# A longer transfer time in the planner's queue model, a new load order, and ten spins ahead of the first transpose

## The chip, the cores and the metric

The kernel runs on one core of one Trainium2 chip. The metric is device time in microseconds (us). Four runs of the kernel before gave 297.55, 297.69, 298.71 and 296.12 us; the median is 297.62 us. A difference of about 1% is what a measurement of this kernel can tell from no change.

## The reference, cut to what matters

Two layers follow each other. The first is a linear recurrence over 768 steps for 4 sequences and 8 heads of 48 elements; the second is a mixture of four experts in which every expert runs on every row:

```python
for t in range(S):                       # r, k, v: (4, 8, 768, 48)
    cur   = einsum('bhd,bhe->bhde', u[None] * kt, vt)
    y[:, :, t] = einsum('bhd,bhde->bhe', rt, state + cur)
    state = w[None, :, :, None] * state + einsum('bhd,bhe->bhde', kt, vt)
x = y as rows: (3072, 384)
p = domain_probs / (domain_probs.sum(-1, keepdims=True) + 1e-09)
for e in range(4):                       # w1: (4, 384, 1024), w2: (4, 1024, 384)
    out += p[:, e:e+1] * (maximum(x @ w1[e], 0.0) @ w2[e])
```

## The kernel before

**Attention.** The 3072 rows are cut into 24 chunks of 128 rows. Chunk `ci` is step `ci // 4` of sequence `ci % 4`, so four neighbouring chunks (a block) belong to four sequences and only chunk `ci + 4` needs the state that chunk `ci` leaves. Each chunk loads three tiles, `Rt`, `Kt` and `Vt` (192 KB each, in rows of 192 bytes; below they are R5, K5, V5 for chunk 5). `scale` multiplies R and K by powers of `w` into `RK`; `T` transposes `RK` (on TensorE with a copy `Tout` for chunks 0 to 7, by a DMA transpose from SyncE's queue for the others); `At` multiplies the two (from chunk 8 on, two chunks at a time); `mask` cuts the triangle; `Y` forms the output from `At`, `Vb` (the bf16 copy of V) and the state; `Yout` adds `dv`, the part of `u`, which GpSimd computes by `ruk_a`, `ruk_b` (with VectorE's sum `dcoef`) and `dv`; `X` transposes the result into `xTe`, the input of the experts (chunks 0 to 7 on TensorE, the others by a DMA transpose `Xout`); `Sm`, `Sv` and `S` renew the state. TensorE's `l1` (lines 596 and 602) forms x @ w1 for a block of four chunks, ScalarE's `relu` (L611, L613) takes it out of PSUM, `l2` (L632) forms h @ w2 chunk by chunk, and `ev` (L640, L642) adds it to `oacc`.

**Weights.** Each of the eight weight matrices comes in three pieces, here `w1e2.0`, `w1e2.1`, `w1e2.2` (576, 576 and 384 KB of f32), is loaded into a slot `wst` and cast to bf16 (`cast`, by ScalarE, VectorE or GpSimd; lines 72 to 76). An `l1` group needs the piece that holds its columns; from the third slot on an `l2` needs all three.

**What sets the order.** No engine decides anything at run time. Each step is a job with an engine, a duration, the jobs that it needs and a rank. When the program is built, a planner (lines 686 to 840) plays the jobs through: an engine that is free takes the ready job of lowest rank. All engines then get their instructions in the planned order, and each engine works through its own queue strictly in that order, so a job whose input is late holds up what stands behind it. All loads, stores and DMA transposes are issued by SyncE, whose jobs are planned in the same way; loads are ranked by their place in the string `ORDER` (L219), which a program outside had searched. The function `dma()` (L690) models the queue behind SyncE: a transfer begins when the one before it has ended, and ends after its duration `us` (0.965 for an R, K or V tile, 0.555 for each 128 rows or columns of a weight piece, 1.1 and 0.45 for DMA transposes). Its result is the time from which the planner lets the jobs that need the transfer begin.

**Spins.** In the first 20 us the planner writes idle matmuls (`spin`, L173) into TensorE's queue. Between two TensorE jobs it puts as many as fit in the gap that the plan shows (L818). The plan gives the products `wmm` and `umm` (L261 and L265: rows of w and u spread over all partitions) 1.65 us each. The first transpose of chunk 0, job `("T", 0, 0)`, is the next job after `umm`; the plan shows no gap between them.

Of the kernel before, what the change touches and what calls it, by code (L numbers as in the profile page):

```python
# [19 lines left out]
def kernel(  # L20
# [129 lines left out]
    def job(name, on, run, needs=(), rank=0.0, takes=(), drops=(), moves=None,  # L150
            behind=()):
        j = Job()
        j.behind = behind
        j.name, j.on, j.run, j.needs, j.rank = name, on, run, list(needs), rank
        j.takes, j.drops, j.moves = takes, drops, moves
        for k in drops:
            tokens[k] = tokens.get(k, 0) + 1
        j.pad = 0.0
        ci = name[1] if isinstance(name, tuple) and name[0] in ATT else -1
        if ci >= SUB:  # L160

            j.pad = PAD_PE if "T" in on else PAD
        j.no = len(jobs)
        assert name not in jobs
        jobs[name] = j
# [3 lines left out]
    def spin(n, m=4):  # L169

        ps = psum.tile([128, 4, 128], F32, tag="mm", bufs=4, name="spin_ps")
        for _ in range(n):
            nc.tensor.matmul(ps[:, 0:m, :], spin_in, spin_in[:, None, :].to_broadcast((128, m, 128)),  # L173
                             start=True, stop=True)
# [40 lines left out]
    def load_p():  # L215
        load_job("prow", (0.36, 2), lambda: nc.sync.dma_start(
            prow, moe_domain_probs.rearrange("(n p) e -> n p e", p=C)))

    ORDER = ("K1 R1 K0 R0 V0 R2 K2 V1 w1e0.1 w1e0.2 K3 w1e0.0 R3 V2 w2e0.0 V3 w2e0.1 w2e0.2 p w1e1.2 "  # L219
             "w1e1.1 R4 w1e1.0 K5 K4 w2e1.0 w2e1.2 w2e1.1 R5 V4 w1e2.2 w1e2.1 K6 w1e2.0 V5 K7 w2e2.2 "  # L220
             "w2e2.1 w2e2.0 R6 V6 K8 V7 R7 w1e3.2 w1e3.0 K9 w1e3.1 w2e3.0 V9 R9 R8 V8 V11 V10 R11 "
             "K10 R10 K12 K11 w2e3.1 V12 w2e3.2 R13 R12 K13 V13 " +
             " ".join(f"c{i}" for i in range(14, TOTC))).split()
    for what in ORDER:
        if what == "p":
# [87 lines left out]
    def attention(ci):  # L313
        b, c = ci % B, ci // B
# [3 lines left out]
        rk = float(ci)  # L318
# [16 lines left out]
        us = 0.48 if ci < SUB else 0.65  # L335
# [33 lines left out]
        def dv():  # L369
            tl["dv", ci] = work.tile([128, H, D], F32, tag="dv", bufs=3, name="dv")  # L370
            nc.gpsimd.tensor_mul(tl["dv", ci], tl["Vt", ci],  # L371
                                 tl["dcoef", ci].to_broadcast((128, H, D)))
        job(("dv", ci), {"P": 0.82}, dv, [("dcoef", ci)], rk - 0.4, (("dv", ci),), (("inp", ci),))

        if dmat:
            def tr():
# [168 lines left out]
    for ci in range(TOTC):  # L545
        attention(ci)
# [136 lines left out]
    avail = {"T": 3.7, "V": 4.5, "A": 3.3, "P": 1.5, "S": 0.6}  # L683


    RING, DMA_LAG, DMA_END = 118, 1.67, 0.7
    queued = []
    expanded = [0.0]

    def dma(now, base, us, nd):  # L690

        taken = max(now + base, expanded[0])
        at = taken
        while True:
            live = [(b, f, n) for b, f, n in queued[-12:] if f > at]
            n_out = sum(n * min(1.0, (f - at) / (f - b)) for b, f, n in live)
            if not live or n_out + nd + 1 <= RING:
                break
            at += 0.05
        expanded[0] = at  # L700
        b = max(taken - base + DMA_LAG, at + 0.4, queued[-1][1] if queued else 0.0)
        queued.append((b, b + us, nd + 1))
        return taken, b + us + DMA_END
    ready_at = {j.name: 0.0 for j in jobs.values()}
    waiting = {e: [] for e in avail}
    events = []
# [15 lines left out]
    now, seq, n_done = 0.0, 1, 0  # L722
# [7 lines left out]
    def start(e):  # L730
# [34 lines left out]
        if j.moves:  # L765
            taken, end = dma(now, us, *j.moves)
            us = taken - now + 0.04
# [15 lines left out]
    while n_done < len(jobs):  # L783
        assert events, "no job can begin"
        now, _, what, x = heapq.heappop(events)
# [25 lines left out]
    with tc.manual_schedule(engines={ET.PE, ET.Pool, ET.DVE, ET.Activation, ET.SP}):  # L811
        spin(NSPIN)
        pe_end = 3.7
        for t, _, e, j in started:
            if e == "T":
                slow = 2.0 if t < 9.0 else 1.0
                n = int((t - pe_end - 0.1) / (0.056 * slow))
                if t < 20 and n > 0:  # L818
                    spin(n, 1)
                pe_end = t + j.on[e] * (2.0 if t < WARM and j.name not in ("wmm", "umm") else 1.0)  # L820
            if len(j.on) > 1 or j.name[0] in ("cast", "Vb", "Tout") or \
                    (j.name[0] == "Xout" and e in "VA"):
                j.run(e)
            else:
                j.run()
# [30 lines left out]
```

## Time and profile before

| | |
|---|---|
| time of the profiled execution | 297.55 us |
| its span, first to last instruction | 295.7 us (1.85 us lie around it) |
| median of four runs | 297.62 us (296.12 to 298.71) |
| TensorE (PE) busy | 285.8 us, 97% |
| weight loads on PE | 169.2 us, 57% |
| VectorE (DVE), ScalarE (ACT), GpSimd (POOL) busy | 153.3, 152.4, 102.9 us |
| granted clock | 1.000 |
| DMA share, 20 to 80 us | 0.96, at 256 GB/s |
| DMA share, 100 to 280 us | 0.34, at 74 GB/s |

A window line gives a stretch of the span, its length, the busy time of PE, of its weight loads, of DVE, ACT and POOL (with the number of instructions), the granted clock, the mean busy share of the 16 DMA engines and the GB/s. A timeline line gives start and duration in us, engine, line, operation, output and inputs, and in brackets how long the engine was idle before and what ended that. A line of waits gives who waited for whom: us in total, times, the longest. "SPq" is SyncE's queue issuing transfers.

### The profile page before, as it was taken

What the parts mean: (1) busy time and instruction counts of PE and PEld (TensorE: products, weight loads), DVE (VectorE), ACT (ScalarE), POOL (GpSimd) and SP (SyncE); (2) the same over time, 40 slices, a digit from 0 to 9 for tenths busy, and PEclk for the clock granted to TensorE, in tenths of its full rate; (3) what the DMA queues carried; (4) which work ended last, traced back from release to release, by engine and by line L of the source; (5) the groups of instructions that cost most, each with busy time, mean ns of one, the idle gap of its engine ahead of it and who ended that gap; (6) DMA issues with size and microseconds to landing.
All of it is one profiled execution on the core that took longest, in us unless ns stands there. A gap on an engine that the chain in (4) does not pass through costs nothing.

```text
span 295.7 us, 5781 instructions
## 1 busy us (share of the span) xinstructions
PE 285.8 (97%) x2264; PEld 169.2 (57%) x2293; DVE 153.3 (52%) x298; ACT 152.4 (52%) x251; POOL 102.9 (35%) x138
## 2 busy tenths in 40 slices
PE   7899999999979999999999999999999999999995
PEld 2787556868735555555555555555555555555553
DVE  5976778697474957536547436545414322101223
ACT  3775958754474443464543564444464444565440
POOL 3783243919849555443522453401000000000000
PEclk9999999999999999999999999999999999999999
DMA  7999889999989497392093383130340100200003
GB/s 151 288 304 298 259 263 304 220 254 192 237 162 177 82 201 179 105 196 46 17 172 88 109 166 70 28 71 29 90 89 0 27 2 27 80 2 0 0 2 106
DMA packets 111199, 37.66 MB, mean 127 GB/s; under 512 B 99242, under 2 KB 111148, under 8 KB 111172
## 3 DMA queue, kind: packets, MB, share of 16 engines
q1 hardware_dynamic: 111156, 37.29, 52.5%
q8 instruction: 18, 0.29, 0.5%
q14 instruction: 9, 0.07, 0.1%
q10 hardware_dynamic: 16, 0.00, 0.0%
HBM read 26.79 MB, written 4.72 MB: 107 GB/s over the span
## 4 chain that ended last, share of the span: by engine, by line
PE 81%; DMA 6%; SPq 6%; POOL 3%; issue 2%; DVE 1%; ACT 1%; POOLq 0%; DVEq 0%
PE out_ps L632 38%; PE hT_ps L602 31%; PE hT_ps L596 5%; SPq L191 4%; DMA wst<-in_moe_w_dram 3%; DMA Vt<-in_v_dram 2%; PE At_ps L436 2%; PE Y_ps L474 1%; DMA Rt<-in_r_dram 1%; PE Y_ps L467 1%; PE St_ps L515 1%; SPq L202 1%; POOL S L535 1%; POOL ruk L353 1%; PE RKT_ps L394 1%
## 5 line engine op out<-in xcount | busy, mean ns | idle before, releaser
L613 ACT ACTIVATE hTs<-hT_ps 128x512 bf16<-128x512 f32 x168 | 99.6, 597 | 94.4 <-PE hT_ps L602 89.4
L632 PE MATMUL out_ps<-w_sb,hTs 128*128 128x384 bf16 x760 | 138.9, 326 | 0.6 <-DVE oacc L642 0.4
L602 PE MATMUL hT_ps<-xTe,w_sb 128*128 128x512 bf16 x475 | 122.0, 379 | 3.0 <-ACT hTs L613 1.6
L632 PEld LDWEIGHTS <-hTs 128*128 128x128 bf16 x760 | 72.6, 98 | 53.7 <-issue 1.0
L642 DVE SCALAR_TENSOR_TENSOR oacc<-out_ps,p_nat,oacc 128x384 f32<-128x384 f32 x71 | 43.8, 617 | 89.8 <-PE out_ps L632 89.5
L602 PEld LDWEIGHTS <-w_sb 128*128 128x128 bf16 x504 | 47.1, 98 | 48.4 <-issue 1.8
L445 DVE TENSOR_TENSOR AtM<-At_ps,mask 128x512 bf16<-128x512 f32 x48 | 30.8, 682 | 16.3 <-PE At_ps L436 16.3
L345 POOL TENSOR_TENSOR ruk<-Rt,Kt 128x384 f32<-128x384 f32 x24 | 24.3, 1017 | 41.5 <-DMA Kt<-in_k_dram 28.7
L371 POOL TENSOR_TENSOR dv<-Vt,dcoef 128x384 f32<-128x384 f32 x24 | 20.4, 853 | 45.5 <-DVE Ysb L483 30.6
L353 POOL TENSOR_TENSOR ruk<-ruk,U_sd 128x384 f32<-128x384 f32 x23 | 23.4, 1020 | 0.9
L640 ACT ACTIVATE oacc<-out_ps,p_nat 128x384 f32<-128x384 f32 x24 | 13.9, 582 | 14.3 <-PE out_ps L632 14.1
L535 POOL TENSOR_TENSOR S<-Tn,wC 64x192 bf16<-64x192 f32 x32 | 18.3, 573 | 5.7 <-DVE Tn L530 4.3
L366 DVE TENSOR_REDUCE dcoef<-ruk 128x8 f32<-128x384 f32 x24 | 13.1, 547 | 13.8 <-POOL ruk L353 13.7
L72 ACT CAST w_sb<-wst 128x1152 bf16<-128x1152 f32 (+1 forms) x13 | 13.6, 1054 | 12.9 <-DMA wst<-in_moe_w_dram 12.9
L596 PE MATMUL hT_ps<-xTe,w_sb 128*128 128x128 bf16 x288 | 18.4, 219 | 0.0
L611 ACT ACTIVATE hTs<-hT_ps 128x512 bf16<-128x512 f32 x24 | 14.2, 597 | 6.5 <-PE hT_ps L596 5.4
L596 PEld LDWEIGHTS <-w_sb 128*128 128x128 bf16 x288 | 16.8, 98 | 0.9
L483 DVE TENSOR_TENSOR Ysb<-Y_ps,dv 128x384 bf16<-128x384 f32 x24 | 13.2, 552 | 5.2 <-PE Y_ps L474 4.3
L332 DVE TENSOR_TENSOR RK<-Kt,W_sd 128x384 bf16<-128x384 f32 x20 | 14.8, 742 | 0.9 <-DMA Kt<-in_k_dram 0.9
L76 POOL CAST Vb<-Vt 128x384 bf16<-128x384 f32 x20 | 10.8, 545 | 9.1 <-PE St_ps L515 3.7
L530 DVE TENSOR_TENSOR Tn<-S,St_ps 64x192 f32<-64x192 bf16 x32 | 11.2, 350 | 3.9 <-PE St_ps L515 3.2
L332 DVE TENSOR_TENSOR RK<-Rt,W_sd 128x384 bf16<-128x384 f32 x20 | 12.7, 636 | 0.3
(67 smaller groups left out, 133.8 us busy)
## 6 DMA issues: line engine op xcount, KB each, us to landing
wst<-in_moe_w_dram SPq DMA_DIRECT2D x16, 576.0 KB, 6.5
Kt<-in_k_dram SPq DMA_DIRECT2D x24, 192.0 KB, 3.8
Rt<-in_r_dram SPq DMA_DIRECT2D x24, 192.0 KB, 3.7
Vt<-in_v_dram SPq DMA_DIRECT2D x24, 192.0 KB, 3.7
out_dram<-oacc SPq DMA_DIRECT2D x23, 192.0 KB, 1.9
wst<-in_moe_w_dram SPq DMA_DIRECT2D x8, 384.0 KB, 5.7
RKT<-RK SPq DMA_TRANSPOSE x16, 3.3
xTe<-Ysb SPq DMA_TRANSPOSE x16, 2.4
```

The costliest lines, as they stand in the source:

```text
L332: eng.tensor_mul(RK[:, i, :, 0:D], tl[("Kt", "Rt")[1 - i], ci], tl["W", i] if ci < SUB and i not in on_pool else W_sd[i])
L345: nc.gpsimd.tensor_mul(tl["ruk", ci], tl["Rt", ci], tl["Kt", ci])
L353: nc.gpsimd.tensor_mul(tl["ruk", ci], tl["ruk", ci], U_sd)
L371: nc.gpsimd.tensor_mul(tl["dv", ci], tl["Vt", ci], tl["dcoef", ci].to_broadcast((128, H, D)))
L445: nc.vector.tensor_mul(tl["AtM", ci][:, j], tl["At", ci, j], mask[:, None, :].to_broadcast((128, NP, C)))
L535: nc.gpsimd.tensor_mul(S_new[pr, :, cl], tl["Tn", ci][pr], wC[pr, :, None].to_broadcast((P2, NP, D)))
L596: nc.tensor.matmul(ps[:, i, :], w1_sb[:, e, db, (fb + i) * 128:(fb + i + 1) * 128], xTe[:, db, s0, :], start=(i == 0 and db == 0), stop=(i ...
L602: nc.tensor.matmul(ps[:, 0:n, :].rearrange("p a b -> p (a b)"), w1_sb[:, e, db, fb * 128:(fb + 1) * 128], xTe[:, db, s0:s0 + n, :].rearran ...
L611: nc.scalar.activation(hTs[:, fb:fb + 4, s0, :], ps, AF.Relu)
L613: nc.scalar.activation(hTs[:, fb, s0:s0 + n, :], ps[:, 0:n, :], AF.Relu)
L632: nc.tensor.matmul(ps, tl["hTs", e, sc][:, fb, s, :], w2_sb[:, e, fb, :], start=(fb == 0), stop=(fb == NFB - 1))
L642: nc.vector.scalar_tensor_tensor(tl["oacc", ci], in0=tl["o", e, ci], scalar=pe, in1=tl["oacc", ci], op0=ALU.mult, op1=ALU.add)
```

## The change

Transfers that are planned after 24 us get 1.06 times their duration in `dma()`; `SLACK` is 0 and adds nothing. `ORDER` is another string. The job `dv` now also names its V tile as needed; the instruction always waited for it. And between `umm` and the first transpose ten spins are written whatever the plan's gap is.

```diff
-    ORDER = ("K1 R1 K0 R0 V0 R2 K2 V1 w1e0.1 w1e0.2 K3 w1e0.0 R3 V2 w2e0.0 V3 w2e0.1 w2e0.2 p w1e1.2 "
-             "w1e1.1 R4 w1e1.0 K5 K4 w2e1.0 w2e1.2 w2e1.1 R5 V4 w1e2.2 w1e2.1 K6 w1e2.0 V5 K7 w2e2.2 "
-             "w2e2.1 w2e2.0 R6 V6 K8 V7 R7 w1e3.2 w1e3.0 K9 w1e3.1 w2e3.0 V9 R9 R8 V8 V11 V10 R11 "
-             "K10 R10 K12 K11 w2e3.1 V12 w2e3.2 R13 R12 K13 V13 " +
+    ORDER = ("K0 V0 R1 R0 K2 K1 R2 w1e0.2 V1 K3 w1e0.1 w1e0.0 R3 V2 w2e0.0 V3 w2e0.1 w2e0.2 p w1e1.1 "
+             "K4 R4 w1e1.2 w1e1.0 w2e1.1 w2e1.0 K5 R5 w2e1.2 w1e2.1 V4 w1e2.2 w1e2.0 V5 w2e2.2 K7 V7 "
+             "w2e2.0 w2e2.1 V6 R6 R7 K6 K8 V8 w1e3.0 w1e3.2 K9 w1e3.1 V9 w2e3.0 R8 V10 K10 R9 R10 "
+             "K12 V11 R11 w2e3.2 K11 R13 V12 w2e3.1 R12 K13 V13 " +
              " ".join(f"c{i}" for i in range(14, TOTC))).split()
...
-        job(("dv", ci), {"P": 0.82}, dv, [("dcoef", ci)], rk - 0.4, (("dv", ci),), (("inp", ci),))
+        job(("dv", ci), {"P": 0.82}, dv, [("dcoef", ci), ("Vt", ci)], rk - 0.4, (("dv", ci),), (("inp", ci),))
...
+    MARGIN, SLACK = 1.06, 0.0
     RING, DMA_LAG, DMA_END = 118, 1.67, 0.7
...
         expanded[0] = at
+        us *= MARGIN if now > 24 else 1.0
         b = max(taken - base + DMA_LAG, at + 0.4, queued[-1][1] if queued else 0.0)
         queued.append((b, b + us, nd + 1))
-        return taken, b + us + DMA_END
+        return taken, b + us + DMA_END + (SLACK if now > 24 else 0.0)
...
                 n = int((t - pe_end - 0.1) / (0.056 * slow))
+                if j.name == ("T", 0, 0):
+                    n = 10
                 if t < 20 and n > 0:
                     spin(n, 1)
```

## The prediction

> **What bounds the kernel now.** I read the windows first, since the mean over the span mixes three stages.
>
> ```profile
> core 0: us, PE busy (x) PEld busy (x) DVE busy (x) ACT busy (x) POOL busy (x), PEclk, DMA share, GB/s
> 5.00:10.00 5.00, 3.59 (x36) 1.93 (x35) 3.05 (x7) 2.84 (x7) 2.60 (x3) 1.00 1.02 202
> 10.00:15.00 5.00, 4.65 (x83) 4.08 (x82) 4.39 (x10) 4.06 (x8) 4.42 (x6) 1.00 1.09 339
> ...
> 20.00:80.00 60.00, 59.66 (x656) 42.05 (x657) 43.91 (x83) 38.98 (x61) 33.35 (x42) 1.00 0.96 256
> 80.00:100.00 20.00, 17.89 (x140) 9.72 (x141) 13.51 (x26) 10.53 (x17) 13.96 (x18) 1.00 0.85 173
> 100.00:280.00 180.00, 178.84 (x1186) 98.12 (x1206) 76.45 (x141) 87.42 (x147) 43.27 (x59) 1.00 0.34 74
> ```
>
> From 20 us on PE is the bound: it lacks 0.34 us of work in 60 us and 1.16 us in the 180 us after 100, but 2.11 us between 80 and 100. In 20 to 80 us the DMA engines are as full as PE (0.96), so there the load order decides what PE can do; after 100 us neither loads nor order have much to give. The list of waits of PE names what its idle time is:
>
> ```profile
> PE hT_ps L602 <- ACT hTs L613: 1.6, 1, 1.6
> PE RKT_ps L394 <- DVE RK L332: 1.1, 1, 1.1
> ...
> PE out_ps L632 <- DVE oacc L642: 0.4, 1, 0.4
> ```
>
> Three waits of size: one at the start (L394, chunk 0's first transpose) and two in 80 to 100 us. The timeline tells what made the 1.6 us; first PE, then ACT:
>
> ```profile
> 84.38 0.81 PE L602 MATMUL hT_ps<-xTe,w_sb 128*128 128x512 bf16 x3 [1.56 <-ACT hTs L613]
> ...
> 80.81 1.15 ACT L72 CAST w_sb<-wst 128x1152 bf16<-128x1152 f32 x1 [2.95 <-DMA wst<-in_moe_w_dram]
> 83.00 0.83 ACT L72 CAST w_sb<-wst 128x768 bf16<-128x768 f32 x1 [1.04 <-DMA wst<-in_moe_w_dram]
> 83.74 2.08 ACT L613 ACTIVATE hTs<-hT_ps 128x512 bf16<-128x512 f32 x4
> ```
>
> ACT stood 2.95 and 1.04 us in front of two casts of the last expert's pieces, which were late; the relus that free PE's PSUM stood behind them in ACT's queue, so PE had no buffer. The data was not needed yet; the queue's order was wrong by about 3 us.
>
> **The margin.** It makes planned transfers 6% longer from 24 us on. Between there and that cast lie, in the old order, 25 input tiles and six matrices. A tile of 196,608 bytes at 202 GB/s (the 5 to 10 us window, inputs alone) is 0.97 us; a matrix of 1.57 MB at 339 GB/s (10 to 15 us, mostly weights) 4.64 us. Together 24.3 + 27.8 = 52 us, and 6% is 3.1 us. This is the size of the 2.95 us wait: the two casts move behind three us of other ACT work, and the relus come first. I take the 1.56 us as gone, and with it the 0.39 us at 97.97, where PE waited for the eviction of a product that ran behind the same hold-up: **−1.95 us**. Bounds: 0 (another late piece takes the place) and −2.11 (all idle time of that window).
>
> What is late next: block 2's `l1` needs the DMA transposes of chunks 8 to 11.
>
> ```profile
> 104.84 1.20 SPq L490 DMA_TRANSPOSE xTe<-Ysb  x1
> ...
> 108.13 1.46 PE L602 MATMUL hT_ps<-xTe,w_sb 128*128 128x512 bf16 x6
> ```
>
> The last of them is issued at 104.84 and lands at 107.35; the second half of the six matmuls, from 108.78, is the first that reads it. Cover 1.4 us. If PE comes 1.95 us earlier and this transpose does not, 0.5 us are given back; I leave that in the range, since the chain before it contains PE's own steps and moves along.
>
> **The order, by counting.** All transfers go through one stream, so what comes earlier puts something else back, by 0.97 us per tile. Tiles ahead of the last piece of each matrix, counted from `p`, before and after: w1e1 1 and 2, w2e1 3 and 4, w1e2 6 and 5, w2e2 8 and 8, w1e3 14 and 15, w2e3 26 and 27. So five of six are within one tile (four later, one earlier). Cost if nothing covers: 0.97 us each for w1e1 and w2e1, where PE's windows of 25 to 50 us show 0.03 to 0.13 us of idle time per 5 us and thus PE just fed: together 0 to +1.9. The first pieces of a matrix arrive in another sequence, which can hide it; the 60 us with 0.34 us idle say that work was always at hand, so I take 0. Chunk 7 is complete two tiles earlier, chunk 6 two later, V4 two later; the pair of chunks 8 and 9 is the one large step, since its last R or K tile goes from the 17th to the 20th place: +2.9 us. Its product needs two DMA transposes behind that on SP (70.04 us, 4.09 us of SP's queue for the two) and ran at 77.17. Moved past one another on SP's queue are only loads and these transposes; the stores begin at 104.
>
> In the first 24 us the last piece of w1e0 stays 12th, R0 4th, R3 and V2 13th and 14th. K1 goes from first to sixth, 5 tiles or 4.9 us: chunk 1's `ruk` on POOL, now at 5.03, moves to about 9 us, into POOL's 1.46 us of waiting for `dcoef` before 9.40. Cover gone, it is up to +1.0 us on POOL, which is busy 4.42 of 5 us there. The second piece of w1e0 comes one tile later, so the first `l1` group (15.11 us) can slip by 1 us; between 16.40 and 17.78 PE runs 15 spins, which that group can fill. I take 0, bounds −2 and +1.
>
> A page's rule here: the Trainium skill, "DMA: Bandwidth & Descriptors", section "Anatomy of one DMA", takes bytes over 436 GB/s as the part that scales. By it a tile would cost an estimated 0.45 us, and every displacement above would be less than half as large. The 202 GB/s window differs from that, and decides.
>
> **The spins.** The row of 17 spins (14.15 us, 1.12 us) gives 66 ns each, ten 0.66 us. The seven spins at the start, four times as wide, took 2.85 us, which is 0.10 us per 128 columns, ten 1.02 us. The gap that they fill is the 1.11 us before L394:
>
> ```profile
> 5.53 0.87 PE L265 MATMUL u_ps<-u_row,ones 128*128 128x384 f32 x2
> 7.51 0.86 PE L394 MATMUL RKT_ps<-ident,RK 128*128 128x128 bf16 x8 [1.11 <-DVE RK L332]
> ```
>
> R0 ends that gap and keeps its place, so both fit: 0. If the tile came earlier than now, up to +0.5 us at the first transpose. The granted clock is 1.00 in every window and the matmuls after the gap run at full pace, so nothing is won in this execution.
>
> The page "TensorE: Matmul & The Clock Gate", section "Part 1: The HAM clock gate", speaks against the spins too: it lowers the clock only after an idle window of about 3.4 us. By it they are worth nothing; a trace in which this gap was paid with a slower clock I do not have, so I keep −1 us as the other end.
>
> **`dv` with its V tile.** One POOL wait of 5.71 us for V4 (before 39.65) can go. POOL idles two thirds of the span and the R5 tile that its next steps need landed at 38.75 anyway: 0, bounds −0.5 and 0.
>
> **Sum.** 297.55 (its median is 297.62, the same) − 1.95 = 295.6; I give **295.7**.
>
> **Rivals.** *The start gets shorter as well.* Between 8 and 18 us the spins fill 5.74 us of PE. V0 comes 2.8 us earlier and w1e0.2 two places; if the first `l1` groups fill the spins at 14.15 (1.12 us) and a third of the 16.40 to 17.78 stretch, PE is saturated 1.5 to 2 us earlier: 293.7. Against it: the last piece of w1e0 and R0 do not move.
>
> *The margin moves the plan, not the time.* Transfers are no faster; the casts wait elsewhere and the relus behind them: 297.6.
>
> *Slower: the pair of chunks 8 and 9 comes late.* Its R9 is 2.9 us later, its two DMA transposes share a full stream (the first took 4.7 us to land where the median is 3.3), and chunk 11 has a weight piece more ahead of its last tile (393 KB at 339 GB/s, 1.2 us). PE's queue holds the pair's `At`, and later its `Y`, at planned places; late, they stop PE outright. With the old stalls kept: 297.6 + 2.9 + 1.2 = 301.7. It decides when the pair is later than the plan has it, that is by more than the 6% of some 43 us (2.6 us) which the margin gives it. For it: `At` of this pair follows its data at once now (77.17). Against: the margin is there just for this.
>
> **Numbers.** Forecast 0.36, own range 294.3 to 297.0 (0.06 of it under 294.6, which is 1% under the median); start shorter 0.26; nothing moves 0.09; pair late 0.29, at 300.7 to 303. Faster by over 1%: 0.06 + 0.26 = 0.32; within 1%: 0.30 + 0.09 = 0.39; slower: 0.29. The range, 293.1 to 302.0, leaves out about 0.07 below and 0.08 above. A 1% is what a measurement can tell.
>
> **What would show it.** The forecast: the waits of PE no longer name hTs L613 with more than 0.5 us, ACT's two waits for wst near 80 us are under 1 us, 80 to 100 us shows PE busy over 19.3 us. The shorter start: spins under 4.5 us and the first L602 or L632 work earlier by over 1 us. The slow case: a PE wait of over 1.5 us at L436, L467 or L596 between 60 and 110 us, released by a DMA transpose or by DVE's mask. The spins: ten L173 matmuls between L265 and L394, which starts no later than 7.6 us. I am wrong if PE is idle at 28 to 40 us for a cast of w1e1 or w2e1, or if the time goes after 110 us.

## The result, and the profile after

The changed kernel takes 296.51 us in the median of 53 runs, the kernel before 297.52 us in the median of 79. The ratio is 0.9966 with a 95% interval of 0.9955 to 0.9978: faster by 1.0 us, or 0.34%. The forecast was 295.7 us. With so many runs a difference of about 0.1% can be told from no change, not only one of 1% as with four. The two profiled executions shown here lie closer together (297.55 and 297.10 us) than the medians.

The profiled execution of the changed kernel took 297.10 us, with a span of 295.3 us. The windows, in the columns shown before:

```profile
core 0: us, PE busy (x) PEld busy (x) DVE busy (x) ACT busy (x) POOL busy (x), PEclk, DMA share, GB/s
5.00:10.00 5.00, 4.49 (x47) 2.82 (x46) 3.02 (x7) 2.81 (x7) 2.31 (x3) 1.00 1.02 219
10.00:15.00 5.00, 4.64 (x82) 4.08 (x81) 4.38 (x10) 3.13 (x7) 4.65 (x6) 1.00 0.89 249
20.00:80.00 60.00, 58.60 (x623) 40.43 (x625) 44.08 (x79) 40.48 (x65) 32.12 (x39) 1.00 0.99 261
80.00:100.00 20.00, 19.89 (x182) 12.00 (x181) 15.11 (x27) 8.64 (x15) 15.52 (x20) 1.00 0.81 149
100.00:280.00 180.00, 178.83 (x1197) 98.32 (x1218) 79.59 (x145) 86.96 (x147) 46.21 (x61) 1.00 0.35 77
```

From 80 to 100 us PE is busy for 19.89 us, where it had 17.89: 2.00 us won. From 20 to 80 us it has 58.60 us, where it had 59.66: 1.06 us lost. From 100 to 280 us the two agree within 0.01 us. The waits of PE in the changed kernel:

```profile
PE hT_ps L596 <- DVE AtM L445: 0.6, 1, 0.6
PE out_ps L632 <- POOL w_sb L76: 0.6, 1, 0.6
PE out_ps L632 <- DVE w_sb L74: 0.5, 1, 0.5
```

The two waits of 80 to 100 us (hTs L613 and oacc L642) are gone. Three new ones stand at 18.8, 26.1 and 39.4 us; the last two are for casts of the first and the second expert's weights. The cast before 39.4 us (of w2e1.0) had itself waited 1.84 us for its load. The timeline shows the start of PE's product work:

```profile
17.16 0.84 PE L596 MATMUL hT_ps<-xTe,w_sb 128*128 128x128 bf16 x12 [0.20 <-ACT w_sb L72]
17.84 0.33 PE L173 MATMUL spin_ps<-spin_in 128*128 128x128 bf16 x3
```

The first group starts at 17.16 us instead of 15.11. This is no accident of one execution: it starts at 14.6 to 15.2 us in all eight traces below that have the old first twelve loads, and at 16.4 to 17.2 us in all six that have the new ones. In 10 to 15 us the DMA engines moved 249 GB/s instead of 339.

### The profile page after: what moved, and what is told of

It is laid out like the page before. It is cut to its first block, busy times and chain, and to the rows that moved or that the text cites. A ratio compares the mean times of both kernels' runs of the same rounds, so it can differ in the third digit from the quotient of the medians.

```text
span 295.3 us, 5795 instructions
## 1 busy us (share of the span) xinstructions
PE 286.5 (97%) x2269; PEld 169.8 (58%) x2298; DVE 158.4 (54%) x300; ACT 150.6 (51%) x249; POOL 105.7 (36%) x138
## 4 chain that ended last, share of the span: by engine, by line
PE 86%; SPq 6%; DMA 5%; issue 1%; DVE 1%; POOL 0%; ACT 0%; ACTq 0%
PE out_ps L632 40%; PE hT_ps L602 35%; DMA wst<-in_moe_w_dram 5%; SPq L191 4%; PE hT_ps L596 4%; PE At_ps L436 2%; PE Y_ps L474 1%; SPq L205 1%; PE Y_ps L467 1%; SPq L202 1%; PE St_ps L515 1%; PE RKT_ps L394 0%; PE out_ps L565 0%; POOL w_sb L76 0%; ACT oacc L640 0%
## 5 line engine op out<-in xcount | busy, mean ns | idle before, releaser
L613 ACT ACTIVATE hTs<-hT_ps 128x512 bf16<-128x512 f32 x168 | 99.8, 598 | 98.9 <-PE hT_ps L602 94.1
L632 PE MATMUL out_ps<-w_sb,hTs 128*128 128x384 bf16 x760 | 138.1, 326 | 1.1 <-POOL w_sb L76 0.6
L602 PE MATMUL hT_ps<-xTe,w_sb 128*128 128x512 bf16 x475 | 121.7, 379 | 1.6
L632 PEld LDWEIGHTS <-hTs 128*128 128x128 bf16 x760 | 72.8, 98 | 54.2 <-issue 1.6
L642 DVE SCALAR_TENSOR_TENSOR oacc<-out_ps,p_nat,oacc 128x384 f32<-128x384 f32 x71 | 43.7, 617 | 91.5 <-PE out_ps L632 90.2
L602 PEld LDWEIGHTS <-w_sb 128*128 128x128 bf16 x504 | 46.9, 98 | 46.7 <-DVE w_sb L74 0.5
L345 POOL TENSOR_TENSOR ruk<-Rt,Kt 128x384 f32<-128x384 f32 x24 | 24.6, 1028 | 45.8 <-DMA Kt<-in_k_dram 25.5
L353 POOL TENSOR_TENSOR ruk<-ruk,U_sd 128x384 f32<-128x384 f32 x23 | 25.5, 1109 | 0.9
L535 POOL TENSOR_TENSOR S<-Tn,wC 64x192 bf16<-64x192 f32 x32 | 17.3, 542 | 6.3 <-DVE Tn L530 4.9
L596 PE MATMUL hT_ps<-xTe,w_sb 128*128 128x128 bf16 x288 | 18.1, 219 | 0.8 <-DVE AtM L445 0.6
L596 PEld LDWEIGHTS <-w_sb 128*128 128x128 bf16 x288 | 16.5, 98 | 1.6 <-ACT w_sb L72 1.1
L332 DVE TENSOR_TENSOR RK<-Kt,W_sd 128x384 bf16<-128x384 f32 x20 | 17.0, 856 | 0.0
L76 POOL CAST Vb<-Vt 128x384 bf16<-128x384 f32 x20 | 11.5, 575 | 15.5 <-DMA Vt<-in_v_dram 6.9
L72 ACT CAST w_sb<-wst 128x768 bf16<-128x768 f32 (+1 forms) x12 | 11.9, 990 | 5.7 <-DMA wst<-in_moe_w_dram 5.7
```

Source lines behind the costliest of these rows:

```text
L332: eng.tensor_mul(RK[:, i, :, 0:D], tl[("Kt", "Rt")[1 - i], ci], tl["W", i] if ci < SUB and i not in on_pool else W_sd[i])
L345: nc.gpsimd.tensor_mul(tl["ruk", ci], tl["Rt", ci], tl["Kt", ci])
L353: nc.gpsimd.tensor_mul(tl["ruk", ci], tl["ruk", ci], U_sd)
L535: nc.gpsimd.tensor_mul(S_new[pr, :, cl], tl["Tn", ci][pr], wC[pr, :, None].to_broadcast((P2, NP, D)))
L596: nc.tensor.matmul(ps[:, i, :], w1_sb[:, e, db, (fb + i) * 128:(fb + i + 1) * 128], xTe[:, db, s0, :], start=(i == 0 and db == 0), stop=(i ...
L602: nc.tensor.matmul(ps[:, 0:n, :].rearrange("p a b -> p (a b)"), w1_sb[:, e, db, fb * 128:(fb + 1) * 128], xTe[:, db, s0:s0 + n, :].rearran ...
```

## How the executions are compared

One profile shows one execution. Of three kernels there are two traces each, and the same load lands 0.2, 0.4 and 2.4 us apart in them (medians over the loads). So beside the measured ratios I use a sum over each trace: every weight load on PE counts with the pace of its product (the time from one to the next in its row: 0.2155 us for L602, 0.1625 for L632, 0.0558 for L596, and so on); this gives PE's work done by a time, whatever order it is done in.

| kernel | ratio to before | work done by 80 us | work from 80 to 105 us |
|---|---|---|---|
| before | 1 | 63.8 | 22.6 |
| ten spins alone | 1.0008 | 62.8 | 22.7 |
| two casts later | 1.0005 | 63.0 | 23.6 |
| new start alone | 0.9992 | 63.3 | 22.9 |
| margin alone | 0.9944 | 63.2 | 24.6 |
| margin alone, again | 0.9959 | 62.3 | 22.8 |
| margin and new start | 0.9973 | 61.8 | 24.4 |
| changed kernel without margin | 1.0017 | 61.4 | 24.3 |
| changed kernel | 0.9966 | 62.0 | 24.9 |
| changed kernel, again | 0.9958 | 62.1 | 24.9 |
| changed kernel without spins | 0.9964 | 63.1 | 24.8 |
| changed kernel, old start | 0.9933 | 62.9 | 24.9 |
| the same, again | 0.9933 | 63.8 | 24.6 |
| the same, K4 and R4 apart | 0.9942 | 62.9 | 24.5 |

"Start" is the first twelve loads. Half an interval is about 0.0025 for the experiments. The two columns of work and the time of the same execution add up to 383.7 to 384.3 us in all fourteen traces: whatever these edits win or lose is won or lost before 105 us.

The work from 80 to 105 us could also look larger only because PE comes later to the same late loads. One trace excludes that as the whole explanation: the changed kernel with the old start has done as much by 80 us as the kernel before (63.8, second trace) and still does 2.0 us more from 80 to 105 us. The ten spins alone, 1.0 us behind at 80 us, win nothing there.

## First experiments: what each part is worth

**The margin alone.** Old order, no ten spins, `dv` as before:

```diff
+    MARGIN, SLACK = 1.06, 0.0
...
+        us *= MARGIN if now > 24 else 1.0
```

> The kernel before with the margin of 1.06 alone: old load order, no ten spins, dv as before. Theory A (the margin puts ACT's casts of the last expert behind the relus): PE's wait of 1.56 us for hTs L613 near 84 us is gone, 80 to 100 us shows PE busy over 19.3 us of 20, and the ratio is 0.993 to 0.996 (1.2 to 2 us faster). Theory B (the gain comes from the new load order, the margin does nothing by itself): ratio 0.999 to 1.003 and the wait stays. Theory C (the gain is the ten spins): the same as B.

Measured: 0.9944 (0.9917 to 0.9971). From 80 to 100 us PE is busy for 19.91 us. PE's waits of this kernel, none of them between 60 and 285 us:

```profile
PE RKT_ps L394 <- DVE RK L332: 1.3, 1, 1.3
...
PE Y_ps L474 <- ACT Vb L72: 0.6, 1, 0.6
PE RKT_ps L394 <- POOL RK L332: 0.3, 1, 0.3
PE hT_ps L596 <- ACT w_sb L72: 0.3, 1, 0.3
```

And ACT where the hold-up was:

```profile
79.80 0.58 ACT L640 ACTIVATE oacc<-out_ps,p_nat 128x384 f32<-128x384 f32 x1 [0.70 <-PE out_ps L632]
80.27 1.88 ACT L72 CAST w_sb<-wst 128x1152 bf16<-128x1152 f32 x2
83.76 0.60 ACT L613 ACTIVATE hTs<-hT_ps 128x512 bf16<-128x512 f32 x1 [1.61 <-PE hT_ps L602]
```

Both casts now run without a wait, and the relus wait for PE, not PE for them. All three signs of theory A came. The margin by itself gives about as much as the whole change; the intervals of the two overlap.

**The change without the margin.**

```diff
-    MARGIN, SLACK = 1.06, 0.0
+    MARGIN, SLACK = 1.00, 0.0
```

> The changed kernel with the margin back at 1.00: new order, ten spins, dv with its V tile. Theory A: the start loss of about 1 us and the emptier DMA stream at 11 to 13 and 27 to 30 us stay, and a wait of PE behind late casts or late tiles of 1 us or more comes back between 60 and 110 us: ratio 1.002 to 1.008, slower than before. Theory B: as the changed kernel, 0.995 to 0.998. Theory C: the same as B.

Measured: 1.0017 (0.9993 to 1.0041), just under what theory A expected, and outside what B and C expected (0.995 to 0.998). Without the margin nothing is left of the gain. The place that theory A named did not show, though: no wait of 1 us came back between 60 and 110 us, and PE did 24.3 us of work from 80 to 105 us. But this trace is a poor witness. It lacks work before 80 us (61.4). PE waited 2.05 us before 19.48 us for a cast of w1e0, and then the granted clock fell by half for over 3 us; two of the four windows:

```profile
21.00:22.00 1.00, 1.00 (x17) 1.00 (x16) 0.09 (x1) 0.48 (x1) 0.88 (x2) 0.50 1.09 270
22.00:23.00 1.00, 1.00 (x13) 1.00 (x11) 0.47 (x1) 0.70 (x2) 0.72 (x1) 0.50 0.98 339
```

The clock averages 0.66, 0.50, 0.50 and 0.63 over the four microseconds from 20 to 24 us, which is some 1.7 us of full pace lost. The margin acts after 24 us, so neither loss is its doing. Three of the 12 executions show a mean clock of 0.993 or 0.994; the median of the other nine is 298.06 us, still no faster than before. PE then came to 80 us with 2.4 us less work done than in the kernel before, and loads that are about 3 us late hold up a late PE less; that this is why no wait came back is likely, but not shown. Where the margin earns its time in the new order is therefore open.

**Two casts later.** A test of the mechanism itself: in the kernel before only the casts w2e3.1 and w2e3.2 are planned 3 us later.

```diff
+    jobs["cast", 2, 3, 1].pad = jobs["cast", 2, 3, 2].pad = 3.0
     left = {j.name: {n for n in j.needs} for j in jobs.values()}
```

> The kernel before, in which the planner lets the two casts w2e3.1 and w2e3.2 (and nothing else) begin 3.0 us after their planned arrival, so that they stand later in an engine's queue. Theory A: the hold-up of the relus behind these two casts is the whole of the 1.56 us and of the 0.39 us at 98 us: both waits go and the ratio is 0.993 to 0.995. If the gain of the changed kernel has another source, or if something else is late right behind, the ratio is 0.998 to 1.002.

Measured: 1.0005 (0.9977 to 1.0032); no gain that can be told from the noise. The relus now run around the casts and the 1.56 us wait is gone, but others stand in 80 to 105 us:

```profile
PE out_ps L632 <- DVE oacc L642: 0.7, 1, 0.7
PE At_ps L436 <- DMA RKT<-RK: 0.3, 1, 0.3
```

The wait for the eviction (0.39 us before) grew to 0.73 us, since PE arrived earlier at a DVE that had stood 2.77 us waiting for POOL's `ruk`; and PE now caught a DMA transpose of the chunks' RK. PE did 23.6 us of work in this stretch, 1.0 us more than before where 2.0 were expected. So the casts were not the only late jobs: taking their wait out let others show. I read it so that what hangs on the loads of that time was planned too early as a whole, and that the margin helps because it moves all of it. No run here moves the other late jobs one by one, so this reading is argued, not shown.

**The spins alone.**

```diff
+                if j.name == ("T", 0, 0):
+                    n = 10
```

> The kernel before with ten spins between u's product and the first transpose, nothing else. Theory A: they lie inside a gap of 1.1 us that R0 ends; ratio 0.999 to 1.001. Theory C (they hold the clock up in executions in which it would fall): ratio under 0.998.

Measured: 1.0008 (0.9983 to 1.0033). In its trace:

```profile
4.95 0.86 PE L265 MATMUL u_ps<-u_row,ones 128*128 128x384 f32 x2
5.65 0.72 PE L173 MATMUL spin_ps<-spin_in 128*128 128x128 bf16 x10
7.40 0.80 PE L394 MATMUL RKT_ps<-ident,RK 128*128 128x128 bf16 x7 [1.03 <-DVE RK L332]
```

The ten take 0.72 us and lie inside the gap. The page of the Trainium skill that the prediction weighed ("TensorE: Matmul & The Clock Gate", section "Part 1: The HAM clock gate") has the clock fall after an idle window of about 3.4 us. For this gap of 1.0 to 1.1 us the traces agree with it: the eight transposes behind the gap take 0.86 us with the ten spins and without them. As a limit for gaps the 3.4 us does not hold here: in the changed kernel without the margin, 2.05 us without a matmul were followed by the half clock shown above, and the measurement decides.

## Second experiments: the start of the order, and two tiles side by side

The changed trace shows stretches in which the DMA engines move little while loads are queued. One is at 27 to 30 us, first before, then after:

```profile
27.00:30.00 3.00, 2.97 (x39) 2.34 (x38) 2.01 (x6) 2.30 (x6) 0.00 (x0) 1.00 1.01 250
```

```profile
27.00:30.00 3.00, 3.00 (x35) 2.32 (x35) 2.46 (x7) 1.11 (x3) 0.00 (x0) 1.00 0.25 65
```

In these 3 us the DMA share falls from 1.01 to 0.25. The changed trace is the extreme case: the six kernels with K4 beside R4 move 65 to 192 GB/s there, the seven with the old order from 24 us on 250 to 314. But the kernel before has a pause of its own 2 us later, behind its two tiles in a row K5 and K4:

```profile
29.00:31.00 2.00, 1.95 (x20) 1.17 (x19) 1.96 (x4) 1.76 (x5) 0.00 (x0) 1.00 0.71 132
```

So the two windows compare a pause with the stretch before one; by 32 us the seven old-order traces have moved 7.79 to 8.14 MB, the six others 7.28 to 7.80. SP's queue in the changed kernel just before:

```profile
21.13 0.79 SPq L191 DMA_DIRECT2D Kt<-in_k_dram  x1
21.96 2.50 SPq L191 DMA_DIRECT2D Rt<-in_r_dram  x1
24.50 4.85 SPq L202 DMA_DIRECT2D wst<-in_moe_w_dram  x2
```

K4 and R4 follow each other, and the issue of the next piece lasts over 4 us while SP waits for no semaphore of that size. V1 and K3 follow each other at 8 us, though there no issue lasts over 2 us. From this came theory D: two tiles in a row, each of 1024 rows, fill what SP's queue can hold, and the stream behind them starts late.

**The new start alone, in the kernel before.**

```diff
-    ORDER = ("K1 R1 K0 R0 V0 R2 K2 V1 w1e0.1 w1e0.2 K3 w1e0.0 R3 ...
+    ORDER = ("K0 V0 R1 R0 K2 K1 R2 w1e0.2 V1 K3 w1e0.1 w1e0.0 R3 ...
```

> The kernel before, in which only the first twelve loads of the order are those of the changed kernel (K0 V0 R1 R0 K2 K1 R2 w1e0.2 V1 K3 w1e0.1 w1e0.0). Theory D (two tiles next to each other fill SP's descriptor queue, so that the next weight piece is issued late and the DMA engines run dry): with V1 and K3 adjacent the traffic falls under 250 GB/s in the mean of 11 to 13 us, as in the two traces with this start (126 and 99 GB/s), and the time grows by 0.4 to 1.2 us, ratio 1.001 to 1.004. Rival E (the start order is worth nothing either way; the first product group fills what were spins, as the prediction has it): ratio 0.999 to 1.001.

Measured: 0.9992 (0.9962 to 1.0023). The dry stretch came (171 GB/s in 11 to 13 us). The median did not grow, which fits rival E, but the interval also holds the 1.001 to 1.004 of theory D.

**The changed kernel with the old start** (the diff above, reversed).

> The changed kernel with the first twelve loads of the kernel before. Theory D: the dry stretch at 11 to 13 us goes, the one at 27 to 30 us (K4 and R4 adjacent) stays; ratio to the kernel before 0.993 to 0.996, under the changed kernel's 0.9966. Rival E: 0.996 to 0.997, like the changed kernel.

Measured: 0.9933 (0.9905 to 0.9961), the lowest ratio of all, as theory D expected; the interval just reaches rival E's 0.996. The windows of 11 to 13 us, the changed kernel first, then this one:

```profile
11.00:13.00 2.00, 1.64 (x29) 1.28 (x27) 1.67 (x5) 1.53 (x3) 2.00 (x3) 1.00 0.66 127
```

```profile
11.00:13.00 2.00, 1.66 (x30) 1.30 (x27) 1.68 (x5) 1.10 (x3) 2.00 (x3) 1.00 1.03 353
```

**K4 and R4 apart as well.**

```diff
-             "K4 R4 w1e1.2 w1e1.0 w2e1.1 ...
+             "K4 w1e1.2 R4 w1e1.0 w2e1.1 ...
```

> The changed kernel with the first twelve loads of the kernel before, and with the piece w1e1.2 moved between K4 and R4. Theory D: the dry stretch at 27 to 30 us goes as well (over 200 GB/s in each of these microseconds), the bytes moved by 30 us are 7.5 MB or more instead of 6.7 to 6.8, and PE has done as much by 45 us as in the kernel before (within 0.5 us). Rival F (the dry stretch comes from the DMA engines themselves, such as one that lags behind the others, and not from which loads stand together): it stays, 6.7 to 7.0 MB by 30 us.

Measured: 0.9942 (0.9916 to 0.9969). The three microseconds:

```profile
27.00:28.00 1.00, 1.00 (x11) 0.68 (x11) 0.86 (x4) 0.00 (x0) 0.00 (x0) 1.00 1.05 242
28.00:29.00 1.00, 1.00 (x13) 0.68 (x10) 0.94 (x4) 0.77 (x2) 0.00 (x0) 1.00 1.02 126
29.00:30.00 1.00, 1.00 (x23) 1.00 (x21) 1.00 (x1) 0.67 (x2) 0.00 (x0) 1.00 0.91 293
```

The DMA share stays at 0.91 or more, where the kernel with only the old start has 0.26 in its first microsecond. But theory D asked for over 200 GB/s in each, and the second has 126. Over the 3 us it is 220 GB/s, against 182 and 192 in the two traces with only the old start. The bytes moved by 30 us are 7.32 MB, not 7.5 (7.10 and 7.17 in those two), and neither PE's work by 45 us (as in the kernel with only the old start) nor the time gained. So the pause moved when the two tiles were taken apart, as theory D says, in one trace; how much is moved in all hardly changed, and theory D's price for this pair was wrong.

**The changed kernel without the spins** (the two lines of the spins taken out).

> The changed kernel without the ten spins. By the theory that they lie in a gap and change nothing: ratio to the kernel before as for the changed kernel, 0.9955 to 0.998. If they hold up the clock or the first transpose: 0.999 or more, or under 0.995.

Measured: 0.9964 (0.9938 to 0.9990), the changed kernel's own ratio. No worth of the spins can be measured in either kernel.

## Third experiments: four kernels on one chip

> The changed kernel itself, beside the next three on one chip. 0.9955 to 0.998 of the kernel before.

Measured: 0.9958 (0.9936 to 0.9981), 296.28 us.

> The changed kernel with the first twelve loads of the kernel before, once more, beside the changed kernel. If the new start costs time (theory D): its median is 0.5 us or more under that of the changed kernel in this call. If not (rival E, for which the kernel before with the new start speaks): within 0.4 us of it.

Measured: 0.9933 (0.9908 to 0.9958), 295.79 us: 0.49 us under the changed kernel, between the two theories' bounds, so neither is decided.

> The kernel before with the margin alone, once more. By the theory that the margin is the whole gain and that the new order gives some of it back: 0.993 to 0.996, at or under the changed kernel of this call. If the first result was luck of that chip: 0.996 to 0.998, like the changed kernel.

Measured: 0.9959 (0.9938 to 0.9980), 296.43 us. The margin gains once more, but 296.43 us is not at or under the 296.28 us of the changed kernel, so this run does not show that the new order gives something back. The profiled execution was the longest of the 12 (298.64 us), and the wait for hTs L613 that the margin had removed is back at half its size, at 87.13 us. So 6% does not cover every execution:

```profile
PE RKT_ps L394 <- DVE RK L332: 2.0, 1, 2.0
...
PE out_ps L632 <- DVE w_sb L74: 0.9, 1, 0.9
PE hT_ps L602 <- ACT hTs L613: 0.8, 1, 0.8
PE Y_ps L467 <- DVE Ysb L483: 0.7, 1, 0.7
```

> The kernel before with the margin and with the first twelve loads of the changed kernel. Theory D: 0.3 to 1 us slower than the margin alone. Rival E: within 0.3 us of it, and then what the changed kernel lacks against the margin alone lies in its order from 24 us on.

This one is the margin alone with the start diff shown above. Measured: 0.9973 (0.9950 to 0.9995), 296.63 us, 0.2 us slower than the margin alone; rival E by the letter.

Taken together, four comparisons of times give for the new start −0.2 us in the kernel before, +0.2 with the margin, and +0.5 and +0.4 us in the changed kernel (the +0.4 against the kernel without spins). PE's work by 80 us is 63.1 us in the mean of the eight traces with the old start and 62.3 in the six with the new one. The traces also say where: by 24 us the new start is 0.7 us of work behind (five traces against eight, without the one at half clock), while from 24 to 80 us the seven traces with the old order and the seven with the new one do the same work, within 0.1 us in the mean. I hold a cost of some tenths of a microsecond for likely and its size for open. Whether the rest of the new order gains anything over the old one is open too: 0.9933, twice, against 0.9944 and 0.9959.

The ratio is lower with the margin in each of the three orders that were run with it and without it: 0.9944 and 0.9959 against 1 in the old one, 0.9973 against 0.9992 with the new start (here the intervals overlap), 0.9966 against 1.0017 in the changed kernel. Only the value 1.06 was run. A margin makes the planner write a different order for every engine, and no run here moved the plan by a similar amount in another way, so how much of the gain is later arrival times as such, and how much a plan that happens to be better, stays open.

The change of `dv` was not run by itself. In the changed trace POOL's wait at that place is not gone: it waits 6.96 us, before 39.75 us, for R5.

## Why the prediction was right in sign and range, and too hopeful in size

*The margin, −1.95 us.* The place was right: the two waits went, and 80 to 100 us gained 2.00 us. The margin alone gave −1.2 to −1.7 us at the end. The working was narrower than the cause: it named two casts behind which the relus stood, and moving just those brought 1.0 us of work at that place and no measurable time. In the changed kernel the larger piece's cast is even done by DVE (at 80.73 us). So that 1.95 came so near to 2.00 is partly luck. The 3.1 us by which the casts were to move is a little large too: in the trace before, R4 and all of w1e1 are issued from 19.31 to 21.06 us, before the margin begins. If the plan has about these times, 24 tiles and five matrices are left, and the same sum gives an estimate of 2.8 us.

*The order, "I take 0", twice.* This is the term that was mis-sized. The last pieces of w1e1 and w2e1 were counted as one tile later each, with 0 to +1.9 us as bounds, and put at 0 because PE had lacked only 0.34 us in 60; the changed kernel lacks 1.40 us there. PE's wait before 39.36 us for a cast of w2e1 is what the prediction had named as a sign that it is wrong (PE idle at 28 to 40 us for a cast of w1e1 or w2e1); it came, at 0.53 us. Over all traces, though, the new order costs no work from 24 to 80 us, so the 0 for these pieces holds in the mean and not in this execution. In the counting, V4 is not two tiles later but fifth among the tiles in both orders, with one weight piece more ahead of it; nothing rests on it. For the start the reasoning was that the first product group slips by one tile and fills spins. It slipped by 2.05 us, in a stream that also paused at 11 to 13 us, and the group behind it by 1.0 us (17.78 to 18.78). Counting tiles ahead of a piece gives its place in the stream, but not the pauses of the stream, and the pauses moved with the order. In the two profiled executions 1.8 us of work lost by 80 us stand against 2.3 us won from 80 to 105 us, which leaves 0.5; their times differ by 0.45 us. In the medians 1.0 us is left of the 1.95 us; of what is missing, only some tenths can be pinned on the start, and the rest stays open.

*What is late next.* I kept 0.5 us for block 2's transposes; the changed trace has no wait there. The transposes moved along, as assumed.

*The spins, 0*, held in both kernels. *`dv`, 0*, was not tested by itself; POOL's wait of 5.71 us for V4 became one of 6.96 us for R5, in line with the reason that was given.

*The page's rate for the transfers.* The 436 GB/s that the prediction set beside its tiles stands in the Trainium skill ("DMA: Bandwidth & Descriptors", section "Anatomy of one DMA") for transfers issued by GpSimd. The loads here are issued by SyncE, so the 0.45 us was no rival price for them.

*The rivals.* The start did not get shorter, it got longer. "The margin moves the plan, not the time" is refuted by the margin alone. The late pair of chunks 8 and 9 did not show: no wait at L436 or L467 between 60 and 110 us in the changed kernel, though R9 came three tiles later in the order. Nor did it show in the same order without the margin, so that the margin is what kept it away is not shown. Where only two casts were moved, a later pair waited 0.3 us for its DMA transpose (L436, at 94.03 us).

## What to carry to other kernels

Where every engine runs a queue that a planner wrote, a job that is planned before its data is there stops all that stands behind it. If the trace shows an engine waiting for loads with needed work queued behind, try correcting the planner's estimate for all loads, not only the one job that shows; here 6%, the only value that was run, was worth 1.2 to 1.7 us and a new load order, searched besides, added nothing that could be measured for certain. And count pauses of the transfer stream as well as bytes when loads are moved.

## What I had not expected of the hardware

The DMA stream pauses although loads are queued. In all fourteen traces there are 11 to 22 half-microseconds between 9 and 70 us in which the core's engines move under 70 KB, where the median is 139 to 148 KB. Two executions of the same kernel have most of them at nearly the same places (the changed kernel near 28, 38, 54, 58 and 69 us both times), so most belong to the program and not to one execution. With the new start the stream is thin at 11 to 13 us: 98 to 184 GB/s in its six traces, 331 to 353 in the eight with the old start. V1 stands beside K3 there, but the twelve loads were exchanged together, so that these two neighbours cause it is not shown. About a third of the low half-microseconds (70 of 219) come 1 to 3 us after a transfer of 16 KB of instructions, which takes 0.9 to 2.5 us of one engine; but a fifth of all half-microseconds lie that near to one, so this is no more than a weak hint, and it was not tested.

The clock also fell after a gap that is short. In the changed kernel without the margin, 2.05 us without a matmul (17.4 to 19.5 us) were followed by half the clock from 20.3 to 23.7 us, and its matmuls of 128 columns then came every 0.107 us instead of 0.056. Several other executions of the record show a mean clock of 0.994 and are among the longer ones of their kernel (five of the changed kernel's, 297.58 to 299.02 us).
